# A listed order for the opening stages, second-block weights split by VectorE, pairs for g, and a moved right side

## Chip, cores and metric

One core of one Trainium2 chip. The metric is the device time of one execution in microseconds (us); lower is better. Beside three timed runs there is one profiled execution, from which every row below comes.

## Reference

```python
a = softmax(phi, axis=seq)                   # (8 batches, 8 heads, 576, 32)
k_m, v_m = a^T k, a^T v                      # 32 memory rows per head
attn = softmax(0.125 * q k_m^T); x = attn v_m        # -> x: 4608 tokens x 512
x = relu(x @ w_in)**2 @ w_out                # block 1, d_ff = 2048
h = x @ w_in2; x = (h - tanh(h)) @ w_out2    # block 2, d_ff = 2048
```

The four weights come as float64, by their bits. Everything else is float32.

## The kernel before

**Arithmetic.** Each fp32 product is three TensorE products of parts: a value is split into a high part (a rounding cast on ScalarE) and a low part (a subtraction, on GpSimd or VectorE), and hi*hi + hi*lo + lo*hi accumulate in PSUM.

**Weights.** `conv` turns a 128x512 tile of float64 into float32: a DMA of 512 KB into a `raw` buffer (L108), an absolute value on ScalarE (L112), four VectorE instructions (L114 to L118). `w1_conv` does so for w_in of block 1 (16 tiles, named by a quarter of d_ff, `fc`, and a pair of heads, `pr`), and stores the result to DRAM for later batches. `wo_conv` does it for w_out (16 tiles) and splits the result (`split`, L148 on ScalarE, L150 on GpSimd). Block 2's 32 tiles are converted and stored during block 1 (`w2_conv`) and loaded and split at its end (`w2_load`).

**Attention.** For each batch, `att_a` (two groups of heads) makes k_m and v_m, and `att_b` (two parities of heads) the softmax over 32 memory rows, which it leaves transposed and split in `aT`. `u_make` multiplies v_m into a quarter of w_in, so block 1's first product is `h = u^T aT` and x is never formed.

**Block 1** runs 256 steps. A step is a unit of 288 tokens (`u`, 16 of them) by one tile of 128 of d_ff (`f`, 16): `l1_mm1` (6 products, L373) three steps ahead, `l1_act` (relu, square, hi cast on ScalarE, lo subtraction on GpSimd, L385 to L391) two steps ahead, `l1_mm2` (12 products, L403 to L405) into four accumulators. The first four units go through in two halves of d_ff, then twelve units whole. Their outputs go to DRAM (`x2_d`).

**Block 2** runs 144 steps, one of 9 groups of 512 tokens by one of 16 tiles of d_ff: `l2_mm1` (12 products, L484), `l2_act` (ScalarE, then six VectorE instructions L499 to L504), `l2_gsplit` (ScalarE L513, GpSimd L514), `l2_mm2` (12 products, L528 to L530). `x2_load` brings the next group's tokens in (L459) and splits them (L465, L468).

**Order.** Every engine runs its instructions in program order, and the program order is the order in which the Python emits. Stages are generators; `at_step` hangs each on a step number, and `tick`, once per step, advances every active generator by one stage if the buffers that it asks for (`free`) are there. For the first two batches these step numbers were written by hand (T0 = -40 on). All DMAs but one kind are issued by the SP queue, in order too.

**Places.** Pools lie on the left or the right side of SBUF, in the order in which they are opened. In the program of before, the tiles of w_out, g, the left x2 and the first 7 `wi` start at multiples of 512 bytes; those of the right side (u, aT; later the other x2 and 9 `wi`) start 384 bytes past one.

Of the kernel before, what the change touches and what calls it, by code (L numbers as in the profile page):

```python
# [9 lines left out]
F32 = mybir.dt.float32  # L10
# [27 lines left out]

W_LO = 2.0 ** -15
# [4 lines left out]
def moe_chain_kernel(ctx: ExitStack, tc: tile.TileContext, q, k, v, phi, w1i, w1o, w2i, w2o, out):  # L44
# [9 lines left out]
    p_s = pool("small", 3)  # L54
# [3 lines left out]
    p_f = pool("wf", 3)  # L58
    ps_a = pool("ps_a", 4, space=PSUM)
# [12 lines left out]
    a_m = pool("a_m", 1, att)  # L72
# [3 lines left out]
    a_vn = pool("a_vn", 1, att)  # L76
# [6 lines left out]
    neg_umax = p_c.tile([P, 32], F32, name="neg_umax")[:, :1]  # L83
# [10 lines left out]
    free = collections.Counter(b=2, f=3, kv=1, ph=1, q=1, e=1, vn=1, vt=2, kt=2, qt=1, sm=1, at=2, w1=2, u=FC)  # L94
# [8 lines left out]
    def conv(src, out, p=None):  # L103
        raw = slot(p or p_raw, [P, 512, 2], "raw", I32)
        dst = raw.rearrange("p n t -> p (n t)")
        if len(src.shape) == 3:
            dst = dst.rearrange("p (c n) -> p c n", c=src.shape[1])
        nc.sync.dma_start(dst, src)  # L108
        yield
        yield "" if out is not None else "f"  # L110
        f = slot(p_f, [P, 512], "wf") if out is None else out
        nc.scalar.activation(f, raw.bitcast(F32)[:, :, 1], AF.Abs)  # L112
        yield
        nc.vector.tensor_scalar(f, f, W_HI, W_LO, op0=ALU.min, op1=ALU.max)  # L114
# [3 lines left out]
        stt(fi, raw[:, :, 0], 29, fi, op0=ALU.logical_shift_right, op1=ALU.bitwise_or)  # L118
        yield
        return f  # L120
# [5 lines left out]
    def w1_conv(fc, pr, p=None):  # L126
        if pr == 0:
            yield "w1"
            w1[0, fc] = slot(p_w, [P, 4, 512], f"w1_{fc}")
        while (0, fc) not in w1:  # L130
            yield
        t = w1[0, fc][:, pr]
        yield from conv(w1i[pr * P:(pr + 1) * P, fc * 1024:(fc + 1) * 1024], t, p)
        done.add(("w", fc, pr))
        yield
        nc.sync.dma_start(w1_d[fc][:, pr], t)

    def w1_load(b, fc):
        yield "w1"
# [7 lines left out]
    def split(f, hi, lo):  # L147
        nc.scalar.copy(hi, f)  # L148
        yield
        nc.gpsimd.tensor_tensor(lo, f, hi.bitcast(F32), op=ALU.subtract)  # L150

    def wo_conv(f, p=None):
        x = yield from conv(w1o[f * P:(f + 1) * P, :], None, p)
        t = slot(p_wo, [P, 2, 512], "wo", F32R)
        yield from split(x, t[:, 0], t[:, 1])
        give("f")
        wo[1, f] = t[:, 0], t[:, 1]
# [5 lines left out]
    def att_a(b, g, p_kv):  # L163
# [3 lines left out]
        nc.sync.dma_start(ph, phi[b, heads].rearrange("h (p c) m -> p h c m", c=NC))  # L167
        kv = []
# [5 lines left out]
        yield  # L174
        yield "e"
        m1 = slot(a_m, [SP, P], "m1")
# [8 lines left out]
        dg = slot(a_m, [P, P], "dg")  # L185
# [12 lines left out]
        s1 = slot(a_m, [SP, 2, P], "s1")  # L198
# [4 lines left out]
        yield "b vn"  # L203
# [6 lines left out]
        give("e")  # L210
        if p_kv is a_kv:
            give("kv")
# [3 lines left out]
        n = slot(a_vn, [P, 2, 2, D], "vn")  # L216
# [7 lines left out]
        give("vn")  # L224
# [14 lines left out]
    def u_make(b, fc):  # L239
        while not {("a", b, g) for g in range(2)} | {("w", fc, pr) for pr in range(4)} <= done:  # L240
# [26 lines left out]
    def att_b(b, o, p_q):  # L267
# [4 lines left out]
        yield  # L272
# [32 lines left out]
        mx = p_s.tile([P, 18], F32, tag="mx9", name="mx9")  # L305
        sm = p_s.tile([P, 18], F32, tag="sm9", name="sm9")
# [28 lines left out]
    def tick(new=()):  # L335
        for gen in new:
            active.append(gen)
            wants[gen] = ""
        for gen in sorted(active, key=lambda gen: wants[gen] != "-"):
            need = collections.Counter(wants[gen].strip("-").split())  # L340
# [17 lines left out]
    seq = [(u, f, a, a + 8) for a in (0, 8) for u in range(4) for f in range(a, a + 8)]  # L358
    seq += [(u, f, 0, FT) for u in range(4, NU) for f in range(FT)]
# [65 lines left out]
    def w2_conv(m, f):  # L425
# [4 lines left out]
        x = yield from conv(src, None)  # L430
# [4 lines left out]
    wi = {}  # L435

    def w2_load(m, f, p, p_x2f):
        x = slot(p_x2f, [P, 512], "w2f")
        nc.sync.dma_start(x, w2_d[m, f])
        yield  # L440
        yield
# [6 lines left out]
        yield from split(x, t[:, 0], t[:, 1])  # L448
# [3 lines left out]
    def x2_load(j, c, p_x2f):  # L452
        ts = [slot(p_x2f, [P, 512], "x2f") for _ in range(2)]
# [13 lines left out]
        for i in range(2):  # L467
            nc.gpsimd.tensor_tensor(lo[:, i], ts[i], hi[:, i].bitcast(F32), op=ALU.subtract)  # L468
            x2[j, c + i] = hi[:, i], lo[:, i]
            yield  # L470
# [74 lines left out]

    T0 = -40
    at_step(T0, att_a(0, 0, a_kv), *(w1_conv(0, pr, p_wo) for pr in range(2)))
    at_step(T0 + 2, *(w1_conv(0, pr, p_wo) for pr in range(2, 4)))
    at_step(T0 + 4, att_a(0, 1, p_wo), att_b(0, 0, a_q))
    for i in range(12):  # L550
        at_step(T0 + 5 + 1.4 * i, w1_conv(1, i - 4, p_wo) if 4 <= i < 8 else wo_conv(i if i < 4 else i - 4, p_wo))
    at_step(T0 + 7, att_b(0, 1, p_u))
    at_step(T0 + 15, u_make(0, 0))
    at_step(T0 + 23, u_make(0, 1))
    at_step(-23, att_a(1, 0, a_kv))
    at_step(-19, att_a(1, 1, p_wo))
    at_step(-15, att_b(1, 0, a_q))
    at_step(-8, att_b(1, 1, p_u))
    at_step(7, u_make(1, 0))
    at_step(8, u_make(1, 1))  # L560
    for i in range(8):
        at_step(-1 + 1.5 * i, wo_conv(8 + i, p_wo if i < 4 else p_raw))
    for i in range(8):
        at_step(10 + 2 * i, w1_conv(2 + i // 4, i % 4))
    at_step(24, u_make(0, 2))
    at_step(33, u_make(1, 2))
    at_step(28, u_make(0, 3))
    at_step(36, u_make(1, 3))
    for b in range(2, B):
        s = 32 * (b - 1) - 14  # L570
        at_step(s, att_a(b, 0, a_kv))
        at_step(s + 8, att_a(b, 1, a_kv))
        at_step(s + 10, att_b(b, 0, a_q))
        at_step(s + 17, att_b(b, 1, a_q))
# [11 lines left out]
    for s in range(T0, N1):  # L586
        if s == N1 - 22:
# [3 lines left out]
            p_x2f = pool("f2", 4, **tile_wise)  # L591
            p_x2.append(pool("x2_0", 4, **tile_wise))
            p_wi += [pool(f"wi{f}", 1, **tile_wise) for f in range(7)]
            for f in range(FT):
                if f < 7:
                    at_step(s + 2 * f, w2_load(0, f, p_wi, p_x2f))
                else:
                    at_step(N1 - 5 + f, w2_load(0, f, p_wi, p_x2f))
                at_step(N1 - 16 + f, w2_load(1, f, p_wo, p_x2f))
            for c in (0, 2):  # L600
                at_step(N1 - 9 + c, x2_load(0, c, p_x2f))
                at_step(N1 + 4 + 3 * (c // 2), x2_load(1, c, p_x2f))
        l1_mm1(s + 3)
        l1_act(s + 2)
        if s >= 0:
            l1_mm2(s)
        if s + 3 == N1 - 1:
            one.close()
            p_x2.append(pool("x2_1", 4, side="right", **tile_wise))
            p_wi += [pool(f"wi{f}", 1, side="right", **tile_wise) for f in range(FT - 1, 6, -1)][::-1]  # L610
        new, plan[s] = plan.get(s, ()), ()
        tick(new)
    plan = {k - N1 - 3: g for k, g in plan.items() if k >= N1}
    for s in range(-3, N2):
        l2_mm1(s + 3)
# [33 lines left out]
```

## Time and profile before

| | us |
|---|---|
| median of 3 runs (lowest, highest) | 1661.2 (1659.74, 1663.03) |
| profiled execution, its own time | 1658.53 |
| its span, first to last instruction | 1656.8 |

The span is what the rows cut up; 1.7 us lie around it. PE is TensorE, PEld its weight loads, DVE VectorE, ACT ScalarE, POOL GpSimd, SPq the DMA queue of SP. A releaser named behind an arrow is what ended a wait.

### The profile page before, as it was taken

How to read it: one execution, taken by the hardware profiler on the slowest of the kernel's cores; microseconds unless marked ns; L12 is line 12 of the kernel's file. 1: busy time of each engine (PE TensorE's matmuls, PEld its weight loads, DVE VectorE, ACT ScalarE, POOL GpSimd, SP SyncE). 2: the span in 40 equal slices, each digit the busy share in tenths (PEclk: the TensorE clock that was granted, in tenths of full speed). 3: DMA queues.
4: the chain of work that ended last, by engine and by line, in shares of the span. 5: the costliest groups of instructions: out<-in, count | busy, mean ns of one | idle time of the engine just before them, and what ended most of it. 6: DMA issues, size and time to landing. Idle time of an engine off the chain costs nothing. (4 is left out here: it accounts for less than half of the span.)

```text
span 1656.8 us, 26399 instructions
## 1 busy us (share of the span) xinstructions
PE 1555.7 (94%) x9904; PEld 1342.5 (81%) x9904; DVE 993.8 (60%) x1482; ACT 840.8 (51%) x1761; POOL 643.6 (39%) x602
## 2 busy tenths in 40 slices
PE   2388999999999999999979999999999999999998
PEld 1167888898989898999968788888888888888886
DVE  5858535354444434430029978787878787777775
ACT  2346566566666565665644443444444444444443
POOL 1346346453444344343655523232323232323322
PEclk9999999999999999999979999999999999999999
DMA  8342746455453635431331010101010101010000
GB/s 274 120 136 85 222 126 179 112 184 162 148 165 113 201 112 187 116 120 63 89 106 49 17 51 1 51 1 51 1 51 1 52 1 52 1 38 14 8 19 26
DMA packets 88705, 145.13 MB, mean 88 GB/s; under 512 B 12288, under 2 KB 64512, under 8 KB 85504
## 3 DMA queue, kind: packets, MB, share of 16 engines
q1 hardware_dynamic: 86272, 141.07, 27.6%
q0 software_dynamic: 2304, 2.36, 1.1%
q8 instruction: 78, 1.28, 0.3%
q14 instruction: 51, 0.42, 0.1%
HBM read 109.58 MB, written 33.82 MB: 87 GB/s over the span
## 5 line engine op out<-in xcount | busy, mean ns | idle before, releaser
L484 PE MATMUL h<-x,wi 128*128 128x512 f32 x1728 | 423.0, 393 | 2.3 <-POOL wi L150 2.3
L514 POOL TENSOR_TENSOR gl<-pl,gh 128x512 fp32r<-128x512 f32 x144 | 192.0, 1334 | 527.6 <-ACT gh L513 527.6
L484 PEld LDWEIGHTS h<-x,wi 128*128 128x128 f32 x1728 | 325.6, 189 | 75.9 <-POOL wi L150 4.0
L391 POOL TENSOR_TENSOR gl<-gg,gh 128x288 fp32r<-128x288 f32 x256 | 223.4, 874 | 387.7 <-ACT gh L390 289.2
L403 PE MATMUL acc<-gh,wo 128*128 128x288 f32 x1024 | 305.3, 298 | 7.8 <-ACT gh L390 6.0
L404 PE MATMUL acc<-gl,wo 128*128 128x288 f32 x1024 | 305.4, 298 | 0.6 <-POOL gl L391 0.6
L405 PE MATMUL acc<-gh,wo 128*128 128x288 f32 x1024 | 305.6, 298 | 0.0
L496 ACT ACTIVATE u<-h 128x512 f32<-128x512 f32 x144 | 86.1, 598 | 398.0 <-PE h L484 397.9
L373 PE MATMUL h<-aT,u 128*128 128x288 f32 x1536 | 259.8, 305 | 13.7 <-ACT r L385 11.0
L373 PEld LDWEIGHTS h<-aT,u 128*128 128x128 f32 x1536 | 218.2, 190 | 48.2 <-ACT r L385 15.6
L528 PE MATMUL o<-wo,gh 128*128 128x512 f32 x576 | 225.2, 391 | 0.0
L530 PE MATMUL o<-wo,gl 128*128 128x512 f32 x576 | 225.1, 391 | 0.0
L529 PE MATMUL o<-wo,gh 128*128 128x512 f32 x576 | 224.2, 389 | 0.0
L403 PEld LDWEIGHTS acc<-gh,wo 128*128 128x128 f32 x1024 | 196.0, 191 | 9.3 <-ACT gh L390 6.5
L404 PEld LDWEIGHTS acc<-gl,wo 128*128 128x128 f32 x1024 | 195.9, 191 | 1.3 <-POOL gl L391 1.3
L405 PEld LDWEIGHTS acc<-gh,wo 128*128 128x128 f32 x1024 | 196.1, 191 | 0.0
L499 DVE SCALAR_TENSOR_TENSOR pl<-u 128x512 f32<-128x512 f32 x144 | 99.6, 691 | 142.7 <-ACT u L496 142.7
L390 ACT CAST gh<-gg 128x288 fp32r<-128x288 f32 x256 | 110.8, 433 | 78.4 <-PE acc L404 72.8
L504 DVE COPY_PREDICATED pl<-m,th 128x512 f32<-128x512 int32 x144 | 141.0, 979 | 4.9
L387 ACT ACTIVATE gg<-r 128x288 f32<-128x288 f32 x256 | 113.9, 445 | 32.9 <-POOL gl L391 9.5
L529 PEld LDWEIGHTS o<-wo,gh 128*128 128x128 f32 x576 | 108.3, 188 | 23.6
L530 PEld LDWEIGHTS o<-wo,gl 128*128 128x128 f32 x576 | 108.1, 188 | 23.4
(84 smaller groups left out, 1964.6 us busy)
## 6 DMA issues: line engine op xcount, KB each, us to landing
w<-w_d SPq DMA_DIRECT2D x24, 1024.0 KB, 5.4
raw<-in_moe_w_in SPq DMA_DIRECT2D x32, 512.0 KB, 6.3
raw<-in_moe_w_out SPq DMA_DIRECT2D x32, 512.0 KB, 4.5
kv<-in_v SPq DMA_DIRECT2D x64, 144.0 KB, 4.1
kv<-in_k SPq DMA_DIRECT2D x64, 144.0 KB, 4.0
q<-in_q SPq DMA_DIRECT2D x16, 576.0 KB, 6.7
x_d<-xs SPq DMA_DIRECT2D x64, 144.0 KB, 1.8
w_d<-wf SPq DMA_DIRECT2D x32, 256.0 KB, 2.2
```

Of the source, the lines that this page charges most:

```text
L373: nc.tensor.matmul(t[:, :HT], uu[:, w, o, c], at[u // 2][:, x, o, u % 2 * HT:u % 2 * HT + HT], start=(n == 0), stop=(n == 5))
L387: nc.scalar.activation(gg, r, AF.Square)
L391: nc.gpsimd.tensor_tensor(gl, gg, gh.bitcast(F32), op=ALU.subtract)
L403: nc.tensor.matmul(o, wh[:, c], gh, start=(f == a), stop=False)
L404: nc.tensor.matmul(o, wh[:, c], gl, start=False, stop=False)
L405: nc.tensor.matmul(o, wl[:, c], gh, start=False, stop=(f == z - 1))
L484: nc.tensor.matmul(t, wi[f][:, w, c, :], x, start=(n == 0), stop=(n == 11))
L504: nc.vector.copy_predicated(pl, m.bitcast(I32), th)
L514: nc.gpsimd.tensor_tensor(lo, pl, hi.bitcast(F32), op=ALU.subtract)
L528: nc.tensor.matmul(o, gh[:, c], wh, start=(f == 0), stop=False)
L529: nc.tensor.matmul(o, gh[:, c], wl, start=False, stop=False)
L530: nc.tensor.matmul(o, gl[:, c], wh, start=False, stop=(f == FT - 1))
```

## The change

The opening follows a list: `ORDER` names 521 moves, each one stage of one generator (`i00` is `att_a` of batch 0, group 0; `j` `att_b`; `w` `w1_conv`; `o` `wo_conv`; `u` `u_make`; `S` the next step of block 1). What can't move yet is put by and tried again before each later move. Units 0 and 1 now go through d_ff in quarters at first (`parts`). `raw`, `wo` and `f2` buffers are counted in `free`. From batch 3 on, attention starts 6 steps earlier and leaves 4 ticks instead of 1 between a load and its use; `w2_conv` leaves 3. Block 2's weights use three pools of landing buffers instead of one, leave 3 ticks, and 22 of the 32 low parts are made by VectorE. gh and gl of block 1 are two halves of one tile, 5 tiles deep (3 pairs before); in block 2 the same pool gives 5 buffers instead of 6. The pad at the right end grows by 96 floats, and the small pools ahead of the weights shrink.

```diff
+ORDER = """
+i00 o2 o11 w02 o3 w22 w03 i00 o0 w00 j11 o1 i01 o12 o8 o0 w00 w02 w02 i00 w10 w00 w02 o0 o6 i00 i00 i21 j00 w01 o0 w23
...
+w01 i11 o10 w13 j00 S S i11 i10 i11 S i11 o3 i11 o3 w12 S j11 i10 o10 o3 S i10 i11 i20 o5 w11 S i11 j11 o6 w10 o8 o4
...
-    p_g = pool("g", 6)
+    p_g = pool("g", 5)
-    pool("pad", 1, side="right").tile([P, 24], F32, name="pad")
+    pool("pad", 1, side="right").tile([P, 120], F32, name="pad")
...
-    def conv(src, out, p=None):
+    def conv(src, out, p=None, ahead=1):
+        yield "wo" if p else "raw"
...
-        yield
+        for _ in range(ahead):
+            yield
...
-    seq = [(u, f, a, a + 8) for a in (0, 8) for u in range(4) for f in range(a, a + 8)]
-    seq += [(u, f, 0, FT) for u in range(4, NU) for f in range(FT)]
+    parts = [(u, a, a + 4) for a in (0, 4) for u in (0, 1)] + [(u, 0, 8) for u in (2, 3)]
+    parts += [(u, 8, FT) for u in range(4)] + [(u, 0, FT) for u in range(4, NU)]
+    seq = [(u, f, a, z) for u, a, z in parts for f in range(a, z)]
...
-        r = slot(p_t, [P, HT], "r")
-        nc.scalar.activation(r, hs.pop(s)[:, :HT], AF.Relu)
         gg = slot(p_t, [P, HT], "gg")
-        nc.scalar.activation(gg, r, AF.Square)
-        gh = slot(p_g, [P, HT], "gh", F32R)
-        gl = slot(p_g, [P, HT], "gl", F32R)
+        nc.scalar.activation(gg, hs.pop(s)[:, :HT], AF.Relu)
+        nc.scalar.activation(gg, gg, AF.Square)
+        g2 = slot(p_g, [P, 2, 320], "g2", F32R)
+        gh, gl = g2[:, 0, :HT], g2[:, 1, :HT]
...
     def w2_load(m, f, p, p_x2f):
-        x = slot(p_x2f, [P, 512], "w2f")
+        of = "f2" if m == 0 else "f" if f < 8 else "raw"
+        yield of
+        x = slot(dict(f2=p_x2f, f=p_f, raw=p_raw)[of], [P, 512], "w2f")
         nc.sync.dma_start(x, w2_d[m, f])
-        yield
-        yield
+        for _ in range(ahead[0]):
+            yield
...
-        yield from split(x, t[:, 0], t[:, 1])
+        yield from split(x, t[:, 0], t[:, 1], nc.gpsimd if m == 0 and f >= 6 else nc.vector)
+        give(of)
...
+    def take(name):
+        if name == "S":
+            if not step_ready(next_step[0]):
+                return False
+            step(next_step[0])
+            active.extend(plan.pop(next_step[0], ()))
+            tick()
+            next_step[0] += 1
+            return True
+        gen = gens[name]
+        return wants[gen] == "end" or advance(gen)
...
-        s = 32 * (b - 1) - 14
+        s = 32 * (b - 1) - 20
...
-                if f < 7:
+                if f < 6:
                     at_step(s + 2 * f, w2_load(0, f, p_wi, p_x2f))
                 else:
-                    at_step(N1 - 5 + f, w2_load(0, f, p_wi, p_x2f))
+                    at_step(N1 - 8 + f, w2_load(0, f, p_wi, p_x2f))
```

## Rows read from the trace of the kernel before

**Rows 1.** The page: busy time, share of the span, instructions of TensorE.

```profile
PE 1555.7 (94%) x9904; PEld 1342.5 (81%) x9904; DVE 993.8 (60%) x1482; ACT 840.8 (51%) x1761; POOL 643.6 (39%) x602
```

**Rows 2.** Busy time by stretch: stretch and length, engines (instructions), granted clock, DMA share, GB/s.

```profile
0.00:105.35 105.35, 42.12 (x337) 23.56 (x337) 67.42 (x118) 29.17 (x55) 27.25 (x32) 1.00 0.68 208
105.35:302.88 197.53, 187.29 (x1578) 171.35 (x1571) 111.30 (x171) 125.05 (x290) 104.00 (x108) 0.98 0.49 138
302.88:815.87 512.99, 505.84 (x4407) 473.55 (x4406) 191.90 (x328) 309.90 (x724) 224.14 (x251) 0.99 0.43 136
815.87:866.96 51.09, 38.52 (x188) 34.17 (x187) 7.80 (x13) 24.20 (x50) 29.92 (x28) 0.77 0.38 110
866.96:936.57 69.61, 67.28 (x290) 53.81 (x289) 64.78 (x78) 34.90 (x62) 41.63 (x28) 1.00 0.15 42
936.57:1651.00 714.43, 714.43 (x3121) 586.04 (x3119) 550.58 (x777) 316.84 (x580) 216.69 (x159) 1.00 0.08 23
```

**Rows 3.** TensorE in order of time: block 1's first product, and two steps running undisturbed.

```profile
105.35 1.66 PE L373 MATMUL h<-aT,u 128*128 128x288 f32 x6
...
812.69 0.96 PE L373 MATMUL h<-aT,u 128*128 128x288 f32 x6
...
815.07 0.96 PE L373 MATMUL h<-aT,u 128*128 128x288 f32 x6
```

**Rows 4.** Stretches, wf tiles alone (w_out's conversions): DVE, ACT, POOL, clock, DMA.

```profile
0.00:105.35 105.35, 23.82 (x32) 10.04 (x16) 10.75 (x8) 1.00 0.68 208
105.35:302.88 197.53, 44.21 (x48) 13.42 (x21) 13.19 (x8) 0.98 0.49 138
```

**Rows 5.** The same for w tiles (w_in's conversions): PE, PEld, DVE, ACT.

```profile
0.00:105.35 105.35, 6.31 (x32) 0.80 (x32) 18.89 (x32) 5.25 (x8) 1.00 0.68 208
105.35:302.88 197.53, 11.83 (x144) 2.02 (x144) 21.61 (x32) 5.37 (x8) 0.98 0.49 138
```

**Rows 6.** A stretch with busy DMA, by engine as in rows 2.

```profile
10.00:35.00 25.00, 6.83 (x61) 4.87 (x61) 16.22 (x30) 6.01 (x10) 3.29 (x4) 1.00 0.92 260
```

**Rows 7.** DMA issues in the first 105.35 us: count, KB each, median us to landing.

```profile
raw<-in_moe_w_out SPq DMA_DIRECT2D x14, 512.0 KB, 6.6
```

**Rows 8.** Waits of TensorE from 302.88 to 815.87: us in total, times, longest.

```profile
PE m1T L182 <- DVE u L252: 4.1, 2, 2.5
```

**Rows 9.** Waits from 815.87 to 866.96, all engines.

```profile
ACT wo L148 <- DMA w2f<-w_d: 13.9, 5, 4.3
ACT x L465 <- DMA x2f<-x_d: 7.8, 2, 4.2
...
PE h L373 <- ACT r L385: 6.0, 3, 3.1
PE acc L403 <- ACT gh L390: 6.0, 2, 3.2
```

**Rows 10.** Waits of SP's queue in the same stretch.

```profile
SPq L439 <- POOL wo L150: 12.0, 6, 4.8
```

**Rows 11.** GpSimd's groups from 815.87 to 936.57: count, busy us, mean ns, idle before.

```profile
L150 POOL TENSOR_TENSOR wi<-w2f,wi 128x512 fp32r<-128x512 f32 x12 | 17.7, 1477 | 0.0
L150 POOL TENSOR_TENSOR wo<-w2f,wo 128x512 fp32r<-128x512 f32 x13 | 16.6, 1281 | 0.0
```

**Rows 12.** VectorE's nearest group to a split, from 105.35 to 302.88.

```profile
L252 DVE TENSOR_TENSOR u<-u,u 128x512 fp32r<-128x512 f32 x17 | 11.0, 683 | 19.7 <-ACT u L251 19.7
```

**Rows 13.** The chain that ended last, in block 2: start, us, what.

```profile
1049.07 2.72 PE h L484 x12
1054.51 2.72 PE h L484 x12
...
1070.95 2.80 PE h L484 x12
1076.50 2.80 PE h L484 x12
...
1115.37 2.79 PE h L484 x12
```

More of the change, by code (lines that the diff above doesn't have):

```diff
@@ L118, in conv @@
         stt(fi, raw[:, :, 0], 29, fi, op0=ALU.logical_shift_right, op1=ALU.bitwise_or)
+        give("wo" if p else "raw")
         yield
@@ L136, in w1_conv @@
         nc.sync.dma_start(w1_d[fc][:, pr], t)
+        done.add(("stored", fc, pr))
     def w1_load(b, fc):
+        while not {("stored", c, pr) for c in range(FC) for pr in range(4)} <= done:
+            yield
         yield "w1"
@@ L239, in u_make @@
     def u_make(b, fc):
-        while not {("a", b, g) for g in range(2)} | {("w", fc, pr) for pr in range(4)} <= done:
+        while not {("a", b, g) for g in range(2)} | {("w", fc, pr) for pr in range(4)} <= done or b > 1 and (b, fc) not in w1:
             yield
@@ L335, in tick @@
     def tick(new=()):
[L336 to L340, printed above, removed]
+        active.extend(new)
+        for gen in sorted(active, key=lambda gen: wants.get(gen, "") != "-"):
+            need = collections.Counter(wants.get(gen, "").strip("-").split())
             if any(free[r] < n for r, n in need.items()):
@@ L469, in x2_load @@
             x2[j, c + i] = hi[:, i], lo[:, i]
+            give("f2")
             yield
@@ L543, in l2_mm2 @@
                     a += n
[L546 to L568, printed above, removed]
@@ new lines, in moe_chain_kernel, with advance, step_ready @@
+    gens.update((f"o{f}", wo_conv(f, p_wo if f < 8 else None)) for f in range(FT))
+    gens.update((f"u{b}{fc}", u_make(b, fc)) for b in range(2) for fc in range(FC))
+    for name, gen in gens.items():
+        wants[gen] = ""
+    def advance(gen):
+        need = collections.Counter(wants[gen].strip("-").split())
+        if any(free[r] < n for r, n in need.items()):
+            return False
+        free.subtract(need)
+        wants[gen] = next(gen, "end") or ""
+        return True
+    def step_ready(s):
+        if s + 3 < N1:
+            u, f, _, _ = seq[s + 3]
+            if (u // 2, f // 4) not in us or not {("b", u // 2, o) for o in range(2)} <= done:
+                return False
+        return s < 0 or (1, seq[s][1]) in wo
@@ new lines, in step @@
+    def step(s):
+        l1_mm1(s + 3)
+        l1_act(s + 2)
+        if s >= 0:
+            l1_mm2(s)
+    next_step = [-3]
+    def take(name):
+        if name == "S":
+            if not step_ready(next_step[0]):
+                return False
+            step(next_step[0])
+            active.extend(plan.pop(next_step[0], ()))
+            tick()
+            next_step[0] += 1
+            return True
+        gen = gens[name]
+        return wants[gen] == "end" or advance(gen)
+    later = []
@@ new lines, in retry @@
+    def retry():
+        k = 0
+        while k < len(later):
+            if take(later[k]):
+                del later[k]
+            else:
+                name = later[k]
+                k += 1
+                while k < len(later) and later[k] == name:
+                    k += 1
+    for b in range(2, B):
+        s = 32 * (b - 1) - 20
+        if b > 2:
+            at_step(s, att_a(b, 0, a_kv))
+            at_step(s + 8, att_a(b, 1, a_kv))
+            at_step(s + 10, att_b(b, 0, a_q))
+            at_step(s + 17, att_b(b, 1, a_q))
@@ L585, in moe_chain_kernel @@
     order.__enter__()
-    for s in range(T0, N1):
+    for name in ORDER.split():
+        retry()
+        if not take(name):
+            later.append(name)
+    while later or next_step[0] < 60:
+        retry()
+        for name in list(gens):
+            if wants[gens[name]] != "end" and name not in later:
+                take(name)
+        if "S" in later or not take("S"):
+            tick()
+    for name, gen in gens.items():
+        if wants[gen] != "end":
+            active.append(gen)
+    for s in range(next_step[0], N1):
         if s == N1 - 22:
@@ L601, in moe_chain_kernel @@
                 at_step(N1 - 9 + c, x2_load(0, c, p_x2f))
[L602 to L606, printed above, removed]
+                at_step(N1 + 4 + c, x2_load(1, c, p_x2f))
+        while not step_ready(s):
+            tick()
+        step(s)
         if s + 3 == N1 - 1:
@@ L609, in moe_chain_kernel, with l2_ready @@
             p_x2.append(pool("x2_1", 4, side="right", **tile_wise))
-            p_wi += [pool(f"wi{f}", 1, side="right", **tile_wise) for f in range(FT - 1, 6, -1)][::-1]
+            p_wi += [pool(f"wi{f}", 1, side="right", **tile_wise) for f in range(FT - 1, 5, -1)][::-1]
         new, plan[s] = plan.get(s, ()), ()
         tick(new)
+    ahead[0] = 1
+    tick(plan.pop(N1, ()))
     plan = {k - N1 - 3: g for k, g in plan.items() if k >= N1}
+    def l2_ready(s):
+        j, f = divmod(s + 3, FT)
+        return (s + 3 >= N2 or f in wi and all((j, c) in x2 for c in range(ET))) and (s < 0 or (2, s % FT) in wo)
     for s in range(-3, N2):
+        while not l2_ready(s):
+            tick()
         l2_mm1(s + 3)
```

77 lines of the change are left out of this document (48 added, 29 removed).

## The prediction

> **What bounds the kernel now.** The page first: TensorE is busy for 94% of the span [rows 1], so what can be won is in stretches where it stands still, runs at the low clock, or takes longer for a product than it need. The table by stretch finds them [rows 2]. Its bounds are block 1's first product (105.35), the second products of block 1's steps 64 (302.88) and 247 (815.87), and of block 2's steps 0 (866.96) and 12 (936.57). To the first bound TensorE works 42 of 105 us and waits for the preparation. From there to 302.88 it stands still for 197.53 - 187.29 = 10.2 us and loses some 3.5 to the low clock (mean 0.98). To 815.87 it stands still for 7.1 us, over half of it behind one attention wait [rows 8]. To 936.57 lie 120.7 us, from 936.57 on it is never idle, and 5.8 us follow the last product.
>
> How long should the 120.7 us be? An undisturbed step of block 1 takes 815.07 - 812.69 = 2.38 us [rows 3], two thirds of it (1.58) second products. The stretch holds 5 whole steps, 4 steps of second products alone, 4 first products of block 2 at 2.72 and 12 of its steps at 5.44: 11.9 + 6.3 + 10.9 + 65.3 = 94.4. So 26.3 us are lost. The table of waits says where: ScalarE stands in order behind loads of weights and tokens (13.9 and 7.8 us), TensorE behind ScalarE [rows 9]; the loads can't be issued sooner since SP waits for GpSimd's subtractions to free the landing buffers [rows 10], and GpSimd makes every low part there at 1.28 to 1.48 us [rows 11].
>
> In block 2 one thing is odd. Twelve first products take 2.72 us in one step and 2.80 in others, and the steps follow each other by 1054.51 - 1049.07 = 5.44 or 1076.50 - 1070.95 = 5.55 us [rows 13]. The first pair is token group 2 with f = 4: x2 and wi both on the left. The second is the same x2 with f = 8, whose wi lies on the right, 384 bytes off. At 1115.37 the token group is 3 (x2 right) and wi is left: 2.79. It is the difference in place that costs, not the side.
>
> **The opening.** In the list, the moves ahead of the first S contain 10 conversions up to their VectorE part (w00 to w03, w13, o0, o1, o2, o12, o3); before, 16 were done by 105.35 (8 of wf, 8 of w). They took VectorE 23.82 + 18.89 = 42.7 us, or 2.67 each [rows 4, 5], of its 67.4 [rows 2]. The other 24.7 us belong to four `att_a`, two `att_b` and two `u_make`; of these eight the list has two, 10 and 5 of 13 moves of a third and fourth, two, and one: 6.15 of 8. That is 19 if all cost alike and 24.7 at most; I take 20. So 26.7 + 20 = 46.7 us of VectorE work stand ahead of the first product in place of 67.4. Loads: 13 raw tiles of 0.52 MB (the 10, and w10 to w12, which ScalarE has touched by then), k and v of three groups (3.5 MB), phi (1.2), q (1.2): 12.7 MB, at 260 GB/s [rows 6] 49 us. So neither bound allows it before about 50; 58 would be VectorE at work for 80% of the time. At the share it had before (67.4 / 105.35 = 64%) it is 73, and if the conversions cost what they cost later, 3.29 ((44.21 + 21.61) / 20) [rows 4, 5], 6 more: 79. I take **66** (a share of 71%): the list mixes the chains of attention with conversions, where before VectorE often had neither.
>
> From there to step 64 I keep **197.5**. Against the 13.7 us that could be won stand about 4 us of TensorE work on batches 0 and 1 that now comes after the first S, 2 of batch 3's that starts 6 steps sooner, and about 8 of waits for VectorE. For by step 32 the list needs 21 more conversions, 21 x 3.29 = 69 us, and perhaps two thirds of the 45.5 us (111.3 - 65.8) that VectorE did besides, 30: 99 us. TensorE needs 35 x 2.38 = 83 and two thirds of its attention (187.3 - 3.5 - 64 x 2.38 = 31.5), 21: 104. They are nearly even, so hiccups show: 0 to 20. The quarters (`parts`) are what makes this possible: units 0 and 1 need only o0 to o3 and w0 for their first 8 steps. They add two rounds of outputs, four VectorE copies at 0.68 or less [rows 12] and as many on ScalarE, hidden behind TensorE's products; 2.7 us if VectorE is the bound just then.
>
> A new wait to look at: o8 to o15, w2 and w3 go through two `raw` buffers. A round is 6.6 us of landing [rows 7], 0.6 on ScalarE (10.04 / 16), 3.3 on VectorE: 10.5, or 5.3 per tile. The list wants 13 of them from step 8 to 32: 68 us, against 24 x 2.38 and 24/64 of the 31.5, 12: 69. It fits, barely. Behind a late load stands ScalarE's order, with the relu of every following step in it, then TensorE.
>
> **The middle.** `w2_conv` leaves 3 ticks and attention 4 from load to use, so ScalarE should wait less: of 7.1 us of standstill I take **4** (0 to 9 with the clock).
>
> **The change of blocks.** 22 low parts go to VectorE, idle there (7.8 of 51 us [rows 2]). Its nearest instruction, with one operand in PSUM, takes 0.68 [rows 12]; from above, GpSimd's 1.28 bounds it. Three landing pools with 8 buffers replace one of 4, so SP's waits for GpSimd and with them ScalarE's 21.7 us of waits mostly go. What is late next: ScalarE itself, 309.9 us over the middle's 183 steps or 1.7 each with attention [rows 2], plus one or two casts of 0.6, about the 2.38 of a step; then the second half of group 0's tokens, which waits for `f2` (3 buffers now) until GpSimd has split the first half. That costs 2 to 5 us at block 2's start. Of 26.3 us lost I let 9 stay: 3 in block 1's tail, 3 there, 3 in the first steps, where VectorE has 64.8 of 69.6 us of work already and gets up to 6 splits. Gain **17.3** (8 to 23).
>
> The Trainium skill speaks against this part: SBUF — State Buffer, section Who interferes with whom, has a VectorE instruction with two SBUF inputs contend with a GpSimd instruction that reads SBUF, one blocking the other whole. The trace agrees with that direction (2.67 against 3.29 us per conversion). With each of the 22 splits at 1.28 in place of 0.68, VectorE does 13 us more, of which by the shares above 3 or 4 would show.
>
> **The right side.** The pad grows by 384 bytes, so the right tiles come to multiples of 512, and so do the left ones, as the pools ahead of them shrink by 512. Then all pairs are of the first kind. From step 12, 128 first and 132 second products of 2.72 remain: 707.2 for 714.4, gain **7.2**. A right pad that missed would gain 0.
>
> **At nothing.** Relu and square in one buffer: same engine, same order. Pairs for g: ScalarE waits less for buffers, behind TensorE, which it feeds three steps ahead. The low half starts 1280 bytes into its pair; if that cost what misplacement costs in block 2 (0.08 / 12 = 7 ns), 1024 products would lose 7 us, but block 1's first products read aT at several offsets and the steps are all 2.38, so 0. In block 2, 5 buffers for 6 make a low part wait for the second products two steps back; three groups of 2.72 us still lie before its use, and it takes 1.3 (cover gone: 1.3 per step). One buffer for the softmax statistics: hidden behind TensorE, under 1 us per batch if not.
>
> **Sum.** 66 + 197.5 + (513 - 4) + (120.7 - 17.3) + 707.2 + 5.8 = 1588.9; with the 1.7 around the span 1590.6. The profiled execution (1658.5) is 2.7 below the median of the runs; I put half of that on: **1592**.
>
> **Rivals.** (1) Place doesn't set the pace; 7 us less gain: 1599. For it: nothing in the rows. The Trainium skill's TensorE: Matmul & The Clock Gate (Back-to-back issue gap) makes the gap a matter of the columns alone, which is this rival. The trace has 227 to 233 ns for the same 512 columns, and its gap would be 216. (2) The opening holds less: first product at 79, and the `raw` rounds a quarter longer than 10.5, 17 us less some slack: 1592 + 13 + 12 = 1617. For it: ScalarE's order, and VectorE even with TensorE. Against: rows 2 show 36% of idle VectorE time to fill. (3) The wait moves at the change of blocks to the token loads or to VectorE, and 13 of the 17 us come back: 1605. (4) Slower: the two `raw` buffers set the pace of steps 8 to 32. To eat the whole gain of 68 us, 13 tiles must take 69 + 68 = 137 us, a round of 21 us in place of 10.5; beyond that it is slower than 1661. For it: one wait in ScalarE's order holds both buffers. Against: a landing takes 6.6 us in the median, with DMA as busy as it gets.
>
> **Chances.** Forecast 0.50, (1) 0.10, (2) 0.22, (3) 0.13, (4) 0.05. Down from 1592, a first product at 58 (8), no waits for VectorE (7), a better middle and change of blocks (9) give 1568; up, case 2 with a little more gives 1622. Left outside are (4), the worst of (2) and a better opening than the bound of 80%. The runs lie within 0.2%, and so much is no change. Only (4) ends above; a sliver of it within 0.2%: faster 0.92, same 0.03, slower 0.05.
>
> **What would show it.** First h product at 58 to 79; step 64 near 264; TensorE idle under 10 us from there to step 247; ScalarE's waits for w2f and x2f together under 8 us; block 2's steps all 5.44 and 12 first products 2.72. Wrong it is if TensorE waits on ScalarE behind `raw` in the first 32 steps, or if steps of 5.55 remain.

## The result and the profile after

The changed kernel takes 1618.97 us in the median (1614.0 to 1620.12, four runs), the kernel before 1660.47 (1659.53 to 1663.03, four runs): a ratio of 0.9742 (0.9718 to 0.9766), 41.5 us less. Forecast were 1592 and a range of 1568 to 1622: the time lies inside, the direction is right, and 27 us of the expected 68 did not come. The profiled execution of the changed kernel is its fastest, 1614.0 with a span of 1611.6. Its other three runs took 4 to 6 us more, with a mean granted clock of 0.988 to 0.990 where the profiled one has 0.993; at which place, no profile here shows. So differences of medians and of traces can lie some us apart.

The table by stretch, cut at the same events as [rows 2] (first product, second products of block 1's steps 64 and 247, of block 2's steps 0 and 12); columns as there:

```profile
0.00:60.57 60.57, 27.54 (x235) 16.75 (x235) 47.57 (x78) 20.86 (x37) 19.80 (x24) 1.00 0.77 249
60.57:287.57 227.00, 200.68 (x1663) 178.15 (x1664) 143.72 (x217) 134.34 (x310) 119.44 (x123) 0.95 0.57 156
287.57:796.35 508.78, 502.95 (x4414) 470.17 (x4413) 209.19 (x335) 318.19 (x727) 215.09 (x245) 1.00 0.43 138
796.35:825.50 29.15, 29.15 (x189) 27.09 (x187) 16.58 (x19) 21.93 (x45) 12.71 (x13) 1.00 0.49 152
825.50:895.49 69.99, 66.70 (x289) 53.65 (x289) 66.95 (x84) 36.70 (x66) 36.25 (x25) 1.00 0.19 53
895.49:1610.00 714.51, 707.95 (x3121) 585.24 (x3119) 595.00 (x778) 317.56 (x581) 220.07 (x161) 1.00 0.09 24
```

Against the forecast's sum, in its order (the fifth term ends with the last product):

| term | forecast | measured | difference |
|---|---|---|---|
| to the first product | 66 | 60.57 | -5.4 |
| to step 64 | 197.5 | 227.00 | **+29.5** |
| to step 247 | 509 | 508.78 | -0.2 |
| to block 2's step 12 | 103.4 | 99.14 | -4.3 |
| to the last product | 707.2 | 710.45 | +3.2 |
| behind it | 5.8 | 5.66 | -0.1 |

One term holds nearly all of the miss. The views say where in it. TensorE's work grew from 187.29 to 200.68, its standstill from 10.2 to 26.3: 7.8 up to step 8, 6.3 up to step 32 and 12.2 after. The time from the first product to the second products of step 8 was 26 us before and is 45.3 now:

```profile
60.57:105.90 45.33, 37.55 (x314) 31.36 (x314) 41.28 (x66) 28.12 (x65) 23.16 (x22) 0.92 0.48 149
105.90:180.69 74.79, 68.44 (x550) 61.18 (x548) 61.94 (x81) 47.69 (x108) 45.04 (x46) 0.98 0.65 171
180.69:287.57 106.88, 94.68 (x802) 85.61 (x803) 40.51 (x72) 58.53 (x138) 51.25 (x57) 0.94 0.54 148
```

VectorE is busy for 41.3 of those 45.3 us and for 61.9 of the next 74.8. TensorE's waits from 60.57 to 287.57, in total, times and longest, are many small ones on the whole chain of preparation, and two large ones:

```profile
PE u L276 <- DVE aT L350: 4.6, 1, 4.6
PE u L276 <- DVE u L281: 3.4, 1, 3.4
PE u L276 <- DVE w L141: 2.7, 1, 2.7
PE acc L431 <- DVE xs L442: 2.6, 2, 1.5
PE h L402 <- ACT aT L354: 2.4, 1, 2.4
PE h L402 <- ACT u L280: 1.9, 2, 1.2
```

From here on the time of step n is that from the second products of step n - 1 to those of step n. The first two waits are one place, step 61, which takes 15.84 us; the third is in step 20, which takes 8.91. In step 61 TensorE makes u for batch 2 out of weights that come back from DRAM, and works at the low clock after the gaps (granted 0.55 in the mean from 265 to 280 us, that is mostly 1.2 GHz). The row of the first wait names the softmax of batch 2 (aT L350), which ended just before; the loads came just as late (the first landed at 268.2, and TensorE went on at 268.3). The queue of SP issues them (L168) late:

```profile
257.99 1.20 SPq L160 DMA_DIRECT2D w_d<-w  x2
259.66 6.51 SPq L168 DMA_DIRECT2D w<-w_d  x2
271.69 0.32 SPq L460 DMA_DIRECT2D w_d<-wf  x1
272.12 4.57 SPq L168 DMA_DIRECT2D w<-w_d  x2
```

Right before the first stand the last stores of w_in tiles (L160): `w1_load` now waits until all 16 are stored, and the list lets the last of them go this late, beside step 58. From 220 to 280 us the queue also stood for their landing:

```profile
SPq L168 <- DMA w_d<-w: 5.8, 1, 5.8
```

At the change of blocks, ScalarE's waits for loads, 13.9 and 7.8 us in [rows 9], are nearly gone:

```profile
ACT wi L175 <- DMA w2f<-w_d: 1.8, 1, 1.8
ACT x L497 <- DMA x2f<-x_d: 1.8, 1, 1.8
ACT wo L175 <- DMA w2f<-w_d: 0.6, 2, 0.4
```

In block 2 the pairs that took 2.80 in [rows 13] take 2.72, and the steps are 5.44 apart. The chain that ended last, three in a row:

```profile
994.11 2.72 PE h L517 x12
...
999.55 2.72 PE h L517 x12
...
1004.99 2.72 PE h L517 x12
```

What is left there are steps 1 to 4 at 6.55 to 6.66 and step 13 of 8.68, where TensorE waits 2.7 us for the low parts of token group 1.

### The profile page after: what moved, and what is told of

The parts are those of the page before. It is cut to its first block, busy times and chain, and to the rows that moved or that the text cites. A ratio compares the mean times of both kernels' runs of the same rounds, so it can differ in the third digit from the quotient of the medians.

```text
span 1611.6 us, 26159 instructions
## 1 busy us (share of the span) xinstructions
PE 1535.0 (95%) x9904; PEld 1331.1 (83%) x9904; DVE 1079.0 (67%) x1508; ACT 849.6 (53%) x1765; POOL 623.4 (39%) x588
## 3 DMA queue, kind: packets, MB, share of 16 engines
q8 instruction: 78, 1.28, 0.3%
## 4 chain that ended last, share of the span: by engine, by line
PE 84%; DVE 10%; issue 2%; DMA 2%; ACT 2%; POOL 1%; DVEq 0%; SPq 0%; ACTq 0%; POOLq 0%
PE h L517 21%; PE h L402 12%; PE acc L431 8%; PE acc L433 8%; PE acc L432 8%; PE o L563 7%; PE o L561 7%; PE o L562 7%; PE u L276 2%; PE vkm L237 1%; DVE pl L536 1%; DVE wf L140 1%; DVE pl L533 1%; PE qT L310 1%; DMA x_d<-xs 1%
## 5 line engine op out<-in xcount | busy, mean ns | idle before, releaser
L517 PE MATMUL h<-x,wi 128*128 128x512 f32 x1728 | 415.2, 389 | 2.7 <-POOL x L500 2.7
L419 POOL TENSOR_TENSOR g<-gg,g 128x288 fp32r<-128x288 f32 x256 | 227.3, 910 | 364.0 <-ACT g L418 276.7
L431 PE MATMUL acc<-g,wo 128*128 128x288 f32 x1024 | 302.2, 295 | 3.0 <-DVE xs L442 2.6
L433 PE MATMUL acc<-g,wo 128*128 128x288 f32 x1024 | 302.3, 295 | 0.0
L432 PE MATMUL acc<-g,wo 128*128 128x288 f32 x1024 | 302.0, 295 | 0.0
L431 PEld LDWEIGHTS acc<-g,wo 128*128 128x128 f32 x1024 | 193.4, 189 | 3.9 <-DVE xs L442 3.0
L432 PEld LDWEIGHTS acc<-g,wo 128*128 128x128 f32 x1024 | 193.2, 189 | 0.0
L433 PEld LDWEIGHTS acc<-g,wo 128*128 128x128 f32 x1024 | 193.2, 189 | 0.0
L414 ACT ACTIVATE gg<-h 128x288 f32<-128x288 f32 x256 | 105.4, 412 | 110.6 <-PE h L402 106.5
L536 DVE SCALAR_TENSOR_TENSOR pl<-pl,u 128x512 f32<-128x512 f32 x144 | 152.4, 1058 | 0.0
```

The source lines that it names most:

```text
L431: nc.tensor.matmul(o, wh[:, c], gh, start=(f == a), stop=False)
L432: nc.tensor.matmul(o, wh[:, c], gl, start=False, stop=False)
L433: nc.tensor.matmul(o, wl[:, c], gh, start=False, stop=(f == z - 1))
L517: nc.tensor.matmul(t, wi[f][:, w, c, :], x, start=(n == 0), stop=(n == 11))
L536: stt(pl, pl, A0, u, op0=ALU.add, op1=ALU.mult)
```

## The experiments

The edits of experiments 6 to 9 leave the list and the work of the opening as they are. In their profiles the first product comes at 60.9 to 62.4 us (60.57 in the changed kernel), step 32 at 181.5 to 183.5 (180.69), and the stretch from the first product to step 64 takes 226.4 to 228.6 us (227.0): so much do these differ from run to run.

**1. Are the late stores the cause of step 61?**

```diff
         done.add(("w", fc, pr))
-        yield
+        if fc < 2:
+            yield
         nc.sync.dma_start(w1_d[fc][:, pr], t)
```

> The stores of the eight w_in tiles of quarters 2 and 3 follow their conversion at once, so that the loads of batch 2's quarters (which wait until all 16 tiles are stored) can be issued near step 41 and not near step 52. Theory A: the 15.84 us of step 61 is TensorE waiting for u of batch 2 behind these late loads (landing 4.8 to 8.5 us, issued at 259.7 and 272.1 us); then step 61 comes down to 3 to 5 us, the low clock after it goes, and the whole is 10 to 15 us faster: 1604 to 1609. Theory B: u of batch 2 is held by the attention chains of batch 2 (VectorE and TensorE stages in order) and the loads are late only because nothing asked sooner; then the wait stays within 3 us of what it is: 1616 to 1619.

1617.98 (1614.05 to 1619.3). Step 61 fell from 15.84 to 9.14, but from step 48 to step 60 it took 2.6 us more, since u for batch 2 is now made among these steps, and step 64 came at 286.92 in place of 287.57. Theory B, though the loads were late as theory A says. TensorE's waits from 225 to 290 us show what came next in line:

```profile
PE h L403 <- ACT aT L355: 3.0, 1, 3.0
PE h L403 <- ACT gg L415: 1.6, 1, 1.6
```

aT is the softmax of batch 2. It ends nearly as late as the weights did.

**2. Is it VectorE's amount of work?**

```diff
-        nc.vector.tensor_scalar(f, f, W_HI, W_LO, op0=ALU.min, op1=ALU.max)
+        if ahead == 3:
+            nc.vector.tensor_scalar(f, f, W_HI, W_LO, op0=ALU.min, op1=ALU.max)
...
-        stt(fi, raw[:, :, 1], -0x40000000, fi, op0=ALU.bitwise_and, op1=ALU.bitwise_or)
+        if ahead == 3:
+            stt(fi, raw[:, :, 1], -0x40000000, fi, op0=ALU.bitwise_and, op1=ALU.bitwise_or)
```

> Leaves out two of the four VectorE instructions of a conversion of block 1's weights (the clamp and the sign; their values are then not the reference's): about 1.3 us less VectorE work in each of 32 conversions, 12 of them ahead of the first product, 9 in steps 0 to 8, and 11 after. Loads, ScalarE, GpSimd and the order of emission stay. Theory A: VectorE, without a gap from 60 to 108 us, sets the pace of steps 0 to 8, which take 38.8 us; with 12 us less work they take 27 to 31, the first product comes 4 to 10 us sooner than 60.6, and the long steps 13, 20 and 33 shrink; 15 to 25 us faster in all: 1594 to 1604. Theory B: the raw buffers and the loads behind them, or the order of the list, set the pace; then the steps stay within 4 us: 1613 to 1619.

1603.98 (1603.29 to 1606.31): theory A's total, but not its place. The first product came at 54.96, 5.6 us sooner with 13.7 us less VectorE work ahead of it (33.9 for 47.6). From it to step 32 it is 118.7 us in place of 120.1, although VectorE's busy time in that stretch fell from 103.2 to 70.0; to step 64 it is 223.3 in place of 227.0. Steps 0 to 8 took 35.0 us (38.8 before), not 27 to 31. So the amount of VectorE's work sets the first product in part, and little of what follows. One place shows why, in VectorE's and then GpSimd's instructions (start, us, what, idle before):

```profile
125.45 5.77 DVE L140 TENSOR_SCALAR w<-w 128x512 int32<-128x512 int32 x1 [1.80 <-ACT w L135]
...
124.82 2.12 POOL L421 TENSOR_TENSOR g<-gg,g 128x288 fp32r<-128x288 f32 x1
125.59 3.83 POOL L179 TENSOR_TENSOR wo<-wf,wo 128x512 fp32r<-128x512 f32 x2
128.10 2.82 POOL L421 TENSOR_TENSOR g<-gg,g 128x288 fp32r<-128x288 f32 x2
129.63 2.68 POOL L179 TENSOR_TENSOR wo<-wf,wo 128x512 fp32r<-128x512 f32 x1
```

An instruction that takes 0.43 us elsewhere took 5.77 while GpSimd ran beside it without a gap; TensorE waited 5.0 us for the VectorE copy behind it, and step 20 took 10.24.

**3. GpSimd beside VectorE.**

```diff
-        yield from split(x, t[:, 0], t[:, 1])
+        nc.scalar.copy(t[:, 0], x)
+        yield
         give("f")
-        wo[1, f] = t[:, 0], t[:, 1]
+        wo[1, f] = t[:, 0], t[:, 0]
```

> Leaves out the low parts of block 1's w_out: the 16 subtractions on GpSimd (21 us) are gone, and the products take the high part in their place, so that TensorE's work is unchanged and the output is not the reference's. VectorE's own work is unchanged. Theory A: VectorE's conversions are long because GpSimd runs beside them (one L139 took 4.09 us, usually 0.43); without these 16 the conversions between the first product and step 32 take 10% less, and step 32 comes 5 to 10 us sooner. Theory B: VectorE's durations do not depend on this, and GpSimd is not what steps 0 to 8 wait for; then step 32 comes within 2 us of 180.7.

1611.36 (1608.88 to 1612.4). Step 32 came at 175.61, 5.1 us sooner, and step 20 took 4.66 in place of 8.91: theory A, at its lower end. From 60 to 180 us VectorE was busy for 97.7 us in place of 103.1, with 148 instructions for 146. From the first product to step 64 it took 221.4 us, 5.6 less. VectorE's L139 on w tiles, from 60 to 182 us, of the changed kernel (count, busy, mean ns, idle before):

```profile
L139 DVE TENSOR_SCALAR w<-w 128x512 int32<-128x512 int32 x12 | 14.3, 1189 | 0.4
```

and without the 16 subtractions:

```profile
L139 DVE TENSOR_SCALAR w<-w 128x512 int32<-128x512 int32 x11 | 10.6, 965 | 0.4
```

**4. The raw buffers** (the forecast's fourth rival, and half of its second).

```diff
-    p_raw = pool("raw", 2)
+    p_raw = pool("raw", 3)
...
-    p_g = pool("g", 5)
+    p_g = pool("g", 4)
```

> A third raw landing buffer, paid for with one of the five pairs for g (the sides stay at multiples of 512 bytes). Theory A: the two raw buffers set the pace from step 8 on, so the stretch from step 8 to step 32 (74.8 us) comes down to 69 or less and the long steps 20 (8.91) and 33 (6.91) shrink; 5 to 10 us faster, 1609 to 1614. Theory B: a raw buffer is free when the list asks for it, and VectorE's order, not the buffer, makes those waits; then no step below 64 changes by more than 1.5 us. In block 2 four buffers in place of five may cost a little, which does not bear on step 64.

`free` counts three raw buffers, too. The result: 1617.22 (1616.88 to 1617.5). From step 8 to 32 it took 76.0 us (74.8 with two), steps 20 and 33 took 9.61 and 6.91: theory B. The number of raw buffers does not set the pace. ScalarE's waits for landings in them, from the first product to step 32 of the changed kernel, come to 4.2 us.

**5. The quarters.**

```diff
-    parts = [(u, a, a + 4) for a in (0, 4) for u in (0, 1)] + [(u, 0, 8) for u in (2, 3)]
+    parts = [(u, 0, 8) for u in range(4)]
```

> Units 0 and 1 go through d_ff in halves again, as before the change; the list stays, and what cannot move yet is put by. Theory A: the quarters are what lets the first eight steps run on four tiles of w_out and one quarter of w_in; without them steps 4 to 7 wait for tiles 4 to 7 and for the second quarter, which come about 20 us after the first product; step 16 is reached 5 to 15 us later and the whole is that much slower: 1624 to 1634. Theory B: VectorE and the attention behind it must do the same work by step 16 in either order; then step 16 comes within 2 us of 128.1.

1628.51 (1627.21 to 1628.66), theory A: step 16 at 144.81 in place of 128.10, step 64 still 13.1 later. In steps 0 to 8 TensorE also works at the low clock (columns as in [rows 2]):

```profile
61.21:124.08 62.87, 44.42 (x314) 34.90 (x315) 43.68 (x70) 27.96 (x63) 24.79 (x23) 0.73 0.40 123
```

**6. VectorE's share at the change of blocks.**

```diff
-        yield from split(x, t[:, 0], t[:, 1], nc.gpsimd if m == 0 and f >= 6 else nc.vector)
+        yield from split(x, t[:, 0], t[:, 1], nc.gpsimd)
```

> All 32 low parts of block 2's weights are made by GpSimd again, as before the change; the three landing pools and the earlier loads stay. Theory A: the gain at the change of blocks (21.6 us) is GpSimd's relief; 22 low parts at 1.28 to 1.48 are 28 to 33 us of GpSimd back where it already does 40 us in 80, so block 1's tail or block 2's first steps wait for weights again: 6 to 17 us slower, 1625 to 1636. Theory B: the landing pools and the earlier loads made the gain, and VectorE's own share costs time in block 2's first five steps (6.6 us each in place of 5.44); then the steps come down to 5.44 and the whole is 3 to 6 us faster: 1613 to 1616.

1617.97 (1615.92 to 1620.67), against 1618.97: neither theory's time, and no change beyond the spread of the runs. In the two traces both effects are there. From block 1's step 255 to block 2's step 0 it takes 16.7 us (12.5 with VectorE), as SP's queue waits for GpSimd's low parts again:

```profile
SPq L469 <- POOL wo L177: 12.9, 7, 3.1
```

but steps 1 to 4 take 6.36, 6.40, 5.77 and 5.44 in place of 6.55 to 6.66, so at step 12 1.9 us of the loss are left. At step 20 it is 4.7, as steps 13 and 14 are longer here; but these vary without such an edit, too (7.7 to 9.1 for step 13 in experiments 7 to 9). Of the 21.6 us gained at the change of blocks most is thus left for the landing pools and the earlier loads, which no run here tried alone.

**7. The right side, back at 384 bytes.**

```diff
-    pool("pad", 1, side="right").tile([P, 120], F32, name="pad")
+    pool("pad", 1, side="right").tile([P, 24], F32, name="pad")
```

> The pad at the right end goes back to 24 floats, so that the right side's tiles start 384 bytes past a multiple of 512 again, and nothing else changes. Theory A (place sets the pace of a product): block 2's steps are 5.55 us again where the two operands lie on different sides, and all is 6.5 to 7.5 us slower: 1625.5 to 1626.5. Theory B (the gap is a matter of the columns alone; what block 2 gained came from other parts): no step changes, within 1 us of 1619.

1624.2 (1621.83 to 1626.63), theory A, a little under its time: steps of 5.53 to 5.57 where the operands lie on different sides, 5.46 where both lie on the right, 5.44 where both lie on the left, and 7.25 us more from step 14 to step 143 (700.85 and 693.60).

**8 and 9. Other distances**: the same pad of 56 floats (256 bytes off) and of 104 (64 off).

> The pad at the right end is 56 floats, so that the right side's tiles start 256 bytes past a multiple of 512, and nothing else changes. Theory A: only places that agree up to a multiple of 512 bytes run at 2.72 us a product group; the mixed pairs cost 2.80 again and the whole is 5 to 7.5 us slower than 1619. Theory B: agreement up to a multiple of 256 (or less) is enough; steps of 5.44 throughout and 1619 within 2 us. A run with 384 bytes had steps of 5.53 to 5.55 and 1624.2.

> The pad at the right end is 104 floats: right side 64 bytes past a multiple of 512, and nothing else changes. Theory A: any difference modulo 512 bytes costs the same 0.08 to 0.11 us a group (steps of 5.53 to 5.55). Theory B: the cost grows or falls with the difference, so 64 bytes give another step than 256 and 384 do; steps between 5.44 and 5.53, or over 5.55. Theory C: agreement up to 64 bytes is enough: 5.44.

With 256: 1615.95 (1615.12 to 1617.24), 693.60 us from step 14 to step 143, as with 0. With 64: 1625.1 (1623.6 to 1626.67), 702.10. So 256 is enough, theory B of the first. With 64 bytes the chain shows three durations:

```profile
985.54 2.76 PE h L517 x12
991.04 2.72 PE h L517 x12
...
1023.68 2.80 PE h L517 x12
```

At 985.54 both operands lie on the right, at 991.04 both on the left, at 1023.68 one on each side. None of the second's theories holds as written: mixed pairs cost the same 2.80 for 64 as for 384, as theory A has it, but nothing for 256; and steps between 5.44 and 5.53 are there (5.49), as theory B has them, but where there is no difference in place. Two operands 64 bytes off together take 2.76, two that are 384 off together 2.73 (the steps of 5.46 in experiment 7).

**10. Batch 2's attention three steps earlier**, with experiment 1's edit and block 2's token group 1 three ticks earlier.

```diff
+    moves, at_s, n_s = [], [], 0
     for name in ORDER.split():
+        n_s += name == "S"
+        moves.append(name)
+        at_s.append(n_s - dict(i2=3, j2=3).get(name[:2], 0))
+    for _, name in sorted(zip(at_s, range(len(moves)))):
+        name = moves[name]
         retry()
...
-                at_step(N1 + 4 + c, x2_load(1, c, p_x2f))
+                at_step(N1 + 1 + c, x2_load(1, c, p_x2f))
```

> Three edits: the stores of w_in follow their conversion at once (as in the first experiment), the listed moves of batch 2's attention come three steps earlier in the list, and block 2's second token group is loaded three ticks earlier. Theory A: step 61 was held by two things that ended nearly together, the late weight loads and the softmax chain of batch 2 (with the loads early, TensorE waited 3.0 us for aT L355 and 0.9 for L357); with both early step 61 comes from 9.1 to under 5 us, and step 13 of block 2 from 8.7 to 5.44; 8 to 13 us faster than the changed kernel, 1606 to 1611. Theory B: a third thing is late just behind (GpSimd's or ScalarE's order); then step 61 stays over 7 us and only the 3.2 us of step 13 are won: 1614 to 1617.

1610.23 (1607.42 to 1611.49), theory A's time. Step 61 took 2.37 us: the loads and the softmax of batch 2 were its two causes. Part of it was given back where the moves now stand: step 8 to step 32 took 79.1 us in place of 74.8 (17.9 from step 20 to 24 in place of 12.2, but 9.9 from 24 to 28 in place of 13.0). Step 64 came 4.9 us sooner than in the changed kernel. Block 2's step 13 did not improve (9.19, then 7.05): an earlier request alone does not help it.

**11. Token halves in a raw buffer, five low parts back on GpSimd**, on top of 10.

```diff
-        yield "f2 f2"
+        by = "raw" if (j, c) == (1, 2) else "f2"
+        yield "raw" if by == "raw" else "f2 f2"
...
-        yield from split(x, t[:, 0], t[:, 1], nc.gpsimd if m == 0 and f >= 6 else nc.vector)
+        yield from split(x, t[:, 0], t[:, 1], nc.gpsimd if f >= (11 if m else 6) else nc.vector)
```

> On top of the version with batch 2's attention earlier (1610.2): the second half of block 2's token group 1 lands in a raw buffer and no longer competes with the weights for the three f2 buffers, and the last five w_out low parts of block 2 go to GpSimd, which is half idle in block 2's first steps (18.8 of 37.4 us) while VectorE is full (35.5). Theory A: steps 13 and 14 of block 2 (9.19 and 7.05 us) waited for low parts of tokens whose load waited for f2 buffers; both become 5.44, and the first steps (6.58, 6.60) lose up to 1 us each; 5 to 8 us faster, 1602 to 1605. Theory B: GpSimd's order (the low parts of g, which wait for the second products before them) holds the token parts however early they land; then steps 13 and 14 keep at least half of their 5.4 us: 1606 to 1611.

1606.7 (1603.89 to 1607.04). Steps 13 and 14 take 5.44, and steps 10 and 11 take 6.51 and 5.99 instead of 5.44 and 5.63, where second products now wait 2.3 us for low parts of g. From step 0 to step 20 it is 113.0 us in place of 118.5. That is theory A in the steps, by two edits that were not run apart; of the time it promised, 3.5 us came.

**12. Only the late moves earlier** (from step 30 on), on top of 11.

```diff
-        at_s.append(n_s - dict(i2=3, j2=3).get(name[:2], 0))
+        at_s.append(n_s - (3 if n_s >= 34 and name[:2] in ("i2", "j2") else 0))
```

> As the version with token halves in raw (1606.7), but only those listed moves of batch 2's attention that stand at step 30 or later come three steps earlier; the ones before stay where the list has them. Theory A: moved with the rest, the exponentials of batch 2 stood in ScalarE's order while VectorE was not ready (ScalarE waited 3.9 us for e L224 at 157.7) and step 23 took 7.2 us; with them back the stretch from step 20 to 24 takes 12.2 us again in place of 17.0 while step 61 stays short: 3 to 5 us faster, 1601.5 to 1604. Theory B: the attention of batch 2 is short of time as a whole, so what is given back at step 23 is lost by step 61 (late aT again): within 1.5 us of 1606.7.

1606.16 (1603.3 to 1607.1, five runs), a ratio to the kernel before of 0.9677 (0.9663 to 0.969). Steps 20 to 24 took 11.8 us again, and steps 24 to 28 16.5 in place of 9.9: theory B. Batch 2's attention costs its time wherever it stands. This version and that of experiment 11 are the fastest whole kernels here, 12 to 13 us under the changed one.

## Why the forecast was right, and where it was not

The time lies inside the range because a first product and a change of blocks better than forecast gave back 9.7 of the 29.5 us by which the second term missed.

**The opening: right, and a little better.** 60.57 for 66, inside 58 to 79 (the 79 adds 6 us of VectorE work to the time as they are; at the share of 64% they would make it 83). VectorE worked 47.57 us ahead of the first product, 46.7 were forecast; it was busy for 79%, close to the 80% taken as the bound. Experiment 2 supports the step in part: 13.7 us less VectorE work moved the first product 5.6 us forward. The other bound, the loads, was put too low in amount and in rate: the core moved 15.1 MB by the first product, not 12.7, at 357 GB/s from 20 to 30 us, not 260. No run holds the two bounds apart.

**The stretch to step 64: the term that failed.** The step was "I keep 197.5": 13.7 us won, against 4 and 2 of moved work and "about 8" of waits. The moved work was sized well. By the groups of TensorE's instructions, attention without u and the first products took 23.0 us there (15.9 before): 7 for the 6. The waits and the low clock were not: 26.3 us of standstill, and 10 us of low clock (13.4 more work less the 7, on top of the 3.5 of before), together 36 for 8, above the forecast's own 0 to 20 for hiccups. The sums of busy time came out near the forecast even here: by step 32 VectorE was busy for 103 us (99 forecast) and TensorE for 106 (104), though both hold time that is not work, VectorE's holds and TensorE's low clock. The error was to set two nearly equal sums side by side and take only a few us for their hiccups, when each engine waits for the other within the step.

Three things are seen in these 36 us. First, VectorE's instructions are held while GpSimd works. The forecast read it as 2.67 against 3.29 us per conversion, an average; the trace has single holds of up to 4 us in the changed kernel, felt by whatever stands behind:

```profile
71.26 4.09 DVE L139 TENSOR_SCALAR w<-w 128x512 int32<-128x512 int32 x1
...
71.02 0.53 POOL L232 TENSOR_TENSOR s<-s 96x128 f32<-96x128 f32 x1
71.51 0.80 POOL L419 TENSOR_TENSOR g<-gg,g 128x288 fp32r<-128x288 f32 x1
72.28 1.27 POOL L177 TENSOR_TENSOR wo<-wf,wo 128x512 fp32r<-128x512 f32 x1
73.51 1.56 POOL L419 TENSOR_TENSOR g<-gg,g 128x288 fp32r<-128x288 f32 x2
```

Experiment 3 took away 16 of GpSimd's instructions and won 5.1 us by step 32, 5.6 of the second term (some of it may be GpSimd's own shorter queue). Second, step 61 (8.0 us of standstill and the low clock behind it), of which the forecast says nothing: it followed the opening only up to step 32 and took the hand-over to batch 2 as it was before. Experiments 1 and 10 show its two causes, and 10 and 12 that removing it wins 5 us, not the 13 by which the step is too long, as the attention that was late there then takes its time earlier. Third, the low clock of 1.2 GHz after the longer gaps: the granted clock is 0.69 from 86 to 94 us and 0.89 from 135 to 150. The experiments price about 6 us for a part of the first and 5 for the second, and halving the conversions (experiment 2) takes 3.7 off the term; what holds the greater part of the 36 is read from the many small waits and not shown by a run.

**The middle: right** (508.78 for 509). Standstill fell by 1.3 us only, [rows 8]'s wait still stands there at 5.8 us, and most of the rest fits the clock (0.99 to 1.00: 2.9 us less busy time for no fewer instructions).

**The change of blocks: right in size (21.6 for 17.3, in 8 to 23), half wrong in its reason.** Waits of ScalarE for loads came to 4.2 us, under the 8 named. But that VectorE takes over 22 low parts was given first place; experiment 6 prices it at 2 to 5 us in the traces and at nothing in the medians. The 22 took VectorE 0.93 us each in the mean (0.67 to 1.78), between the 0.68 of the forecast and the 1.28 of its counter-argument. What was to be late next was right: VectorE in the first steps (four of 6.6, where the forecast's sign was 5.44 throughout), and the second half of a token group behind `f2`, though of group 1 and not 0; experiment 11, with its two edits, supports that.

**The right side: right to the tenth.** From step 12 to the last product 710.45, of which 3.24 are the one long step: 707.2, as forecast, and every other step is 5.44. Experiment 7 undoes it alone, so rival 1 is out. The rule in the Trainium skill on which that rival stood (TensorE: Matmul & The Clock Gate, Back-to-back issue gap) has no place for it, and the measurement decides against it. But "multiples of 512" was too narrow: 256 serve as well (experiment 8). And "the difference in place that costs, not the side" is not all of it: two operands that agree, but lie 64 bytes past, are slower too (2.76).

**The other rivals.** (2) gave 1617, nearly the time measured, by a mechanism that did not happen: first product at 79, raw rounds a quarter longer. Experiment 4 rules out the raw ring, and (4) with it. (3) did not happen. Of the forecast's signs, step 64 near 264 failed (287.6).

## What to carry to other kernels

When a schedule makes two engines' sums nearly equal, price the waits by the longest hold that the trace shows on either, not by the mean of a shared resource, and follow the list up to where the regular order takes over. A late event often has a second cause that ends just behind the first: after removing one, read what the same wait names next before trusting the gain. Here operands that are multiplied together did best when both started at multiples of 256 bytes; it costs a pad and gave 7 us.

## What the runs showed of the hardware

**VectorE beside GpSimd.** Of the conversion instructions of the changed kernel that start before 300 us, by their starts and ends, those that no GpSimd instruction overlaps (by 0.05 us or more) took 0.41, 0.43, 0.69 and 0.72 us in the mean (L137, L139, L140, L141; 17, 20, 15 and 17 of them), those that one overlaps 0.65, 1.29, 1.13 and 1.25 (20, 17, 21 and 19). Without overlap they hardly vary (L139: 0.43 to 0.45 in all 20), so it is not that long instructions only meet more of GpSimd's. By these differences 39 us of VectorE's time go to it (20 x 0.24 + 17 x 0.86 + 21 x 0.44 + 19 x 0.53). The subtraction of u (L281), whose one operand is in PSUM, takes 0.68 either way. The Trainium skill's SBUF — State Buffer, Who interferes with whom, describes an exclusive lock, held for a whole instruction, in which one-input VectorE instructions of the copy and tensor_scalar kind can take part as well as those with two SBUF inputs. The trace agrees as to who is held, L139 with one input most of all (0.43 to 4.09, and 5.77 for the same instruction in experiment 2); but the holds shown above outlast one GpSimd instruction, the 4.09 us five of them in a row.

**Place and TensorE's pace.** Twelve first products took 2.72 us with both operands at multiples of 256 bytes, 2.80 with one of them 64 or 384 past, 2.76 with both 64 past and 2.73 with both 384 past. Why is open; distances between 64 and 256 were not tried.
